# Block 0's attention sums as float32 products on TensorE, with a new order of all operations

## The chip, the cores and the metric

The kernel runs on one core of a Trainium2 chip. The core has a matrix engine (TensorE, called PE; its weight loads are shown apart as PEld), three engines for elementwise work (VectorE or DVE, ScalarE or ACT, GpSimd or POOL), and SyncE (SP), which here only issues DMAs. SBUF is the memory on the chip in which tiles lie, over 128 partitions; PSUM is the smaller one into which PE writes its products. Each engine runs its own list of instructions in order and waits on semaphores for the others. The metric is the time of one execution on the device in microseconds (us).

## The reference

Three steps follow one another on 8192 tokens (2 batches of 4096) of width 192:

```python
# 1: causal local attention, 7 taps, 8 heads of 24 channels
w = softmax(weight_gen, axis=-1)                     # per token and head, over the 7 taps
x_pad = concat([zeros(B, 6, D), x], axis=1)
out[b, s, h, :] = sum_k w[b, s, h, k] * x_pad[b, s + k, h*24:(h+1)*24]
# 2: h = x @ w_in (192 -> 2048); x = silu(h) @ w_out (2048 -> 192)
# 3: h = x @ w_in2
P = a0 + a1*h + a2*h**2 + a3*h**3
Q = 1 + |b0|*|h| + |b1|*h**2
out = (P / (Q + 1e-6)) @ w_out2
```

The weights of the two MLPs arrive as 64-bit floats.

## The kernel before, in words

**Tiling.** Token 64p + j lies on partition p at position j. The work is cut into 16 blocks of 4 positions, 512 tokens each. A block b goes through attention, MLP 1 (eight units, two hidden tiles of 128 each), and MLP 2 (the same). Numbers are split into a rounded part and a rest ("hi", "lo"), both in the format fp32r, and a product of two is made of three or so of their products.

**The order.** Every operation has a name and sits in one long list, ORDER, from which the program is issued; the order on each engine is the order of the list. `name@1` picks the second of the engines that the operation may run on, `:c` names the slot that its new tile takes (25 slots in SBUF, four of two banks each in PSUM, named A to D), and `^` marks ahead of a name load one of four function tables on ACT. Nothing else decides the order.

**Names.** X.b loads x's window of 10 positions for block b (Z.0 is the second half of block 0's: positions of the block itself; X.0 alone is the six positions that precede it, from the partition before). s0l, s0m, s0d, s0e, s0t, s0n are load, maximum, subtraction, exponential, sum and normalization of the softmax of a chunk of weights; s1 is the next chunk. For each position j, M (taps 0 to 3, 768 wide) and m (taps 4 to 6, 576 wide) multiply x by the weights (L580), p and r add (576 and 384 wide, L590 and L594), and a makes the last sum, 192 wide, into the tile ao (L600). AD copies the last 64 channels of ao beside themselves; T transposes ao to channels-by-tokens in PSUM (L628, L630); XH and XL make the hi and lo parts (L654, L658). In block 0 two groups of transposes whose results are overwritten run on PE as well: W0 (64, L635), which needs x, and W1 (16, L613), which needs a0 and ends ahead of the first multiplication, since A0.0 takes the same PSUM tile.

**The MLPs.** A0 to A7 and C0 to C7 are the two products of MLP 1 by unit, S, H and L its elementwise steps (silu, hi, lo); B, D, and U, V, u, w, Y, N, G, g, h, l are those of MLP 2; EC, EM, EA and FC, FT, FE, FA, O carry a block from MLP 1 to MLP 2 and out. A0.0 is thus the first multiplication of the MLPs; each unit's A has ten matmuls, six with the hi part of x (the second needs the lo part of the weights, q0A0x) and four with the lo part.

**The weights.** An operation name that begins with q is a step of decoding a weight tile: q0A0l0 and l1 load (MLP 0, matrix part A, tile 0), a0 and a1 and 40 and 41 put the number together from its 16-bit words on ACT (L448) and DVE (L461), h and x make hi (L477, L499) and lo (L482). All of it happens in the first 80 us, in between the rest.

Of the kernel before, what the change touches and what calls it, by code (L numbers as in the profile page):

```python
# [29 lines left out]
K = 7  # L30
# [19 lines left out]
    q1B0a1 q1B040:B a0.1:o X.2 C4.0 q1A1l1:b S6.0 q1B041 s3l:d a3.1 q0O3x q1A0a0 q1O3l1:m p1.1@1 q1B0h0 H6.0:g  # L50
    q1B0x0 a2.1 s2n@1 q1A0a1 L6.0:r A7.0:D q1B0h1 r1.1@1 s2s C5.0 q1O2l0:c q1A040:A a1.1 S7.0 q1A041 q1B0x1 C6.0
    H7.0:j q1O0a0 L7.0:e q1O0a1 AD.1@1 T.1:B q1A0h q1O040:D q1O041 C7.0 q1O1a0 q1A0x q1O0h q1O1a1 q1O0x XH0.1:q
    q1O140:A EC.0:w q1O141 EM.0 XL0.1:y A2.1:D q1O1h q1A1a0 q1O1x AW.2 q1A1a1 q1O3l0:p q1A140:B A1.1:A AW.3 S2.1
    q1A141 q1A1h@1 H2.1:s m3.2:u L2.1:n S1.1 M3.2:x q1O2a0 EA.0 A0.1:D H1.1:g q1A1x M2.2:r XH1.0:h L1.1:o A3.1:B
# [5 lines left out]
    L5.1:m H4.1:u r0.3@1 A6.1:D S7.1 L4.1:r m2.3:b H7.1:o Y3.0 p2.3@1 B4.0:C S6.1 L7.1:k g0.0 a3.2 C4.1 ^^U4.0:q  # L60
    h2.0@2:y N3.0 AD.2 h0.0@2:b B6.0:A V4.0:l Y1.0 H6.1:x u4.0 N1.0 C5.1 l0.0@1:r w4.0 M3.3:u L6.1:t T.2:C ^^^G3.0
    C6.1 U6.0:f g3.0 XH0.2:m Y4.0 G1.0 D0.0:D g5.0 g1.0 ^^^^s3e C7.1 XL0.2:n h1.0:e V6.0:t l1.0@1:x A0.2:C EC.1@1:c
    u6.0 EM.1 ^^N4.0 l2.0@1:b w6.0 D1.0 ^S0.2 h5.0:r H0.2:a EA.1 B7.0:A XH1.1:k L0.2:o XL1.1:s A3.2:C V7.0:p
    h3.0@2:e U7.0:x l3.0@1:c B1.1:B u7.0 S3.2 w7.0 D2.0 ^^^V1.1:h Y6.0 G4.0 H3.2:i B2.1:A g4.0 Y7.0 h4.0:j D3.0
# [5 lines left out]
    w5.1 ^S4.2 m1.4:o M2.4@1:t A6.2:A S7.2 r2.3@1 H7.2:j m2.4:v C3.2 S6.2 L7.2:m p1.4@1 H4.2:n B7.1:C L4.2:o h3.1:b  # L70
    ^^^G0.1 a2.3 r1.4 G2.1 C4.2 g0.1 H6.2:i Y5.1 h0.1:g V7.1:a B6.1:D g2.1 U7.1:n r0.4@1 G1.1 L6.2:o C5.2 AD.3 g1.1
    ^^N5.1 u7.1 B4.1:A h1.1:w U6.1:h p2.4@1 w7.1 V6.1:d C6.2 U4.1:p r2.4@1 Y6.1 V4.1:k l0.1@1:s T.3:C h2.1@1:v u6.1
    C7.2 XH0.3:i w6.1 N6.1 a0.4:o XL0.3:e D0.1:D M3.4:f u4.1 ^^^G6.1 l1.1@1:y EC.2@1:j A3.3:C G5.1 w4.1 EM.2 g5.1
    A0.3:A ^S3.3 g6.1 h5.1:m H3.3:g EA.2 D1.1 L3.3:s XH1.2:l l2.1@1:q S0.3 XL1.2:d H0.3:j B0.2:C Y4.1 l3.1@1:w
# [838 lines left out]
```

## Time and profile before

| | us |
|---|---|
| median of 3 runs | 1238.34 (1237.13 to 1238.6) |
| profiled execution | 1237.37 |
| its span (first to last instruction) | 1235.6 |
| PE busy | 1208.8 (98%) |
| ACT busy | 1107.3 (90%) |
| DVE busy | 1061.5 (86%) |
| POOL busy | 703.7 (57%) |

The profile is of one execution. Busy times of engines overlap each other. The view by stretches gives each engine's busy time between two moments, with the number of instructions; what PE lacks to the length of the stretch is its idle time. In a timeline a row gives the start, the time from the start to the end of the last of the merged instructions, the engine, the line of the kernel, the operation, and the tiles; in brackets stands the idle time ahead of it and what ended it. Instructions of one engine overlap a little, so that the distance from start to start is shorter than a row's own time.

### The profile page before, as it was taken

To read this page: it belongs to the slowest core of one execution; us is meant where nothing else is said; L and a number is where in the kernel's file an instruction comes from. 1 tells how busy PE (TensorE), PEld (TensorE's weight loads), DVE (VectorE), ACT (ScalarE), POOL (GpSimd) and SP (SyncE) were. 2 spreads that over 40 slices of the span, in tenths; PEclk is the share of its full clock that TensorE was granted. 3 is DMA by queue.
4 is the path that set the end of the run, shared out by engine and by line. 5 is a ranking of instruction groups with operands and counts; after the bars stand their busy time and mean duration, and the time that the engine had idled before them with its cause. 6 is when DMAs were issued, how large, how long until landed. Compare 5 with 4: busy or idle time off the path is not lost.

```text
span 1235.6 us, 14545 instructions
## 1 busy us (share of the span) xinstructions
PE 1208.8 (98%) x5456; PEld 997.3 (81%) x5456; DVE 1061.5 (86%) x954; ACT 1107.3 (90%) x1053; POOL 703.7 (57%) x455
## 2 busy tenths in 40 slices
...
DMA packets 18998, 45.15 MB, mean 37 GB/s; under 512 B 3828, under 2 KB 10354, under 8 KB 18928
## 3 DMA queue, kind: packets, MB, share of 16 engines
...
q8 instruction: 43, 0.70, 0.2%
q14 instruction: 27, 0.22, 0.1%
...
## 4 chain that ended last, share of the span: by engine, by line
PE 86%; DVE 6%; ACT 5%; issue 2%; DMA 1%; POOL 1%; SPq 0%; ACTq 0%; DVEq 0%; POOLq 0%
PE h L678 43%; PE acc L709 8%; PE acc L705 8%; PE acc L710 8%; PE acc L706 8%; PE acc L707 8%; ACT L878 1%; PE to L834 1%; DVE y L786 1%; DVE g1l L730 1%; ACT y L791 1%; ACT y L794 1%; ACT y L771 1%; DVE t L777 1%; DVE dec L461 1%
## 5 line engine op out<-in xcount | busy, mean ns | idle before, releaser
L807 POOL TENSOR_TENSOR g2l<-t,g2h 128x1024 fp32r<-128x1024 f32 x95 | 247.4, 2611 | 162.8 <-DVE g2h L317 93.7
L678 PE MATMUL h<-xh,wa 128*128 128x512 f32 x1024 | 317.7, 391 | 4.3 <-DVE g1l L730 1.8
L315 POOL TENSOR_SCALAR g2h<-t 128x1024 fp32r<-128x1024 f32 x84 | 108.7, 1298 | 232.2 <-DVE t L797 209.3
L678 PEld LDWEIGHTS h<-xh,wa 128*128 128x128 f32 x1024 | 190.4, 188 | 49.3 <-issue 4.2
L878 ACT ACT_TABLE_LOAD x167 | 214.3, 1283 | 3.7 <-PEq L897 0.7
L786 DVE SCALAR_TENSOR_TENSOR y<-y,b_sb 128x1024 f32<-128x1024 f32 x128 | 185.8, 1459 | 22.9 <-ACT y L771 22.6
L678 PE MATMUL h<-xl,wa 128*128 128x512 f32 x512 | 199.4, 389 | 0.4 <-DVE xl L658 0.4
L678 PE MATMUL h<-xh,wb 128*128 128x512 f32 x512 | 199.4, 389 | 0.0
L678 PE MATMUL h<-xl,wb 128*128 128x512 f32 x512 | 199.3, 389 | 0.0
L730 DVE TENSOR_TENSOR g1l<-h,g1h 128x1024 fp32r<-128x1024 f32 x128 | 155.6, 1219 | 46.0 <-ACT g1h L726 42.7
L777 DVE TENSOR_TENSOR t<-t,h 128x1024 f32<-128x1024 f32 x128 | 155.3, 1214 | 39.9 <-ACT t L767 26.1
L797 DVE SCALAR_TENSOR_TENSOR t<-t,a_sb,y 128x1024 f32<-128x1024 f32 x128 | 174.5, 1378 | 16.2 <-ACT y L794 15.9
L580 POOL TENSOR_TENSOR pr<-xw,aw 128x768 f32<-128x768 f32 (+1 forms) x99 | 153.2, 1558 | 32.6 <-DMA aw<-wsm 10.9
L780 DVE SCALAR_TENSOR_TENSOR t<-t,a_sb,h 128x1024 f32<-128x1024 f32 x128 | 163.5, 1279 | 8.2 <-ACT y L771 4.9
L722 ACT ACTIVATE h<-h 128x1024 f32<-128x1024 f32 x128 | 129.5, 1012 | 40.1 <-PE h L678 34.9
L767 ACT ACTIVATE t<-h,a_sb 128x1024 f32<-128x1024 f32 x128 | 153.4, 1202 | 13.1 <-PE h L678 11.9
L771 ACT ACTIVATE y<-h,b_sb 128x1024 f32<-128x1024 f32 x128 | 141.9, 1112 | 20.0 <-PE h L678 14.1
L791 ACT ACTIVATE y<-y,c_sb 128x1024 f32<-128x1024 f32 x128 | 144.4, 1148 | 10.5 <-DVE y L786 9.8
L726 ACT ACTIVATE g1h<-h 128x1024 fp32r<-128x1024 f32 x128 | 131.1, 1027 | 6.4 <-POOL ao L600 1.3
L794 ACT ACTIVATE y<-y 128x1024 f32<-128x1024 f32 x128 | 131.0, 1054 | 0.6
L678 PEld LDWEIGHTS h<-xl,wa 128*128 128x128 f32 x512 | 96.1, 188 | 20.9 <-DVE xl L658 0.9
L678 PEld LDWEIGHTS h<-xh,wb 128*128 128x128 f32 x512 | 96.1, 188 | 20.3
...
## 6 DMA issues: line engine op xcount, KB each, us to landing
...
```

Of the source, the lines that this page charges most:

```text
L580: e.tensor_tensor(out=p.rearrange("p k (h g) -> p k h g", g=G), in0=st[xw][:, j + k0:j + k0 + n, :].rearrange("p k (h g) -> p k h g", g=G) ...
L678: pe.matmul(out=h[:, i], lhsT=w[:, f], rhs=xx, start=(terms is first and n == 0), stop=(terms is second and n == 1),)
L730: dve.tensor_tensor(out=t, in0=st[hb], in1=st[gh].bitcast(F32), op=ALU.subtract)
L767: act.activation(out=q, in_=st[hb], func=AF.Identity, scale=a_sb[:, 3:4], bias=a_sb[:, 2:3])
L771: act.activation(out=q, in_=st[hb], func=AF.Abs, scale=b_sb[:, 1:2])
L777: dve.tensor_tensor(out=st[t], in0=st[t], in1=flat(), op=ALU.mult)
L780: dve.scalar_tensor_tensor(out=st[t], in0=st[t], scalar=a_sb[:, 1:2], in1=flat(), op0=ALU.add, op1=ALU.mult)
L786: dve.scalar_tensor_tensor(out=st[y], in0=st[y], scalar=b_sb[:, 0:1], in1=st[y], op0=ALU.add, op1=ALU.mult)
L791: act.activation(out=st[y], in_=st[y], func=AF.Ln, scale=c_sb[:, 0:1], bias=1e-6)
L797: dve.scalar_tensor_tensor(out=st[t], in0=st[t], scalar=a_sb[:, 0:1], in1=st[y], op0=ALU.add, op1=ALU.mult)
L807: e.tensor_tensor(out=q, in0=st[t], in1=st[gh].bitcast(F32), op=ALU.subtract)
L878: act.preload_act_table((None, AF.Silu, AF.Ln, AF.Sigmoid, AF.Exp)[k])
```

## The change

For block 0 the operations a, AD, T and W1 go. In their place K0 to K3 run on PE: for each position j, the two partial sums that r leaves are each multiplied by the identity in float32, and PSUM adds them. That gives the transposed sum in one step; the last 64 channels are multiplied twice, once for either half of the partitions, which is what AD's copy was for. A K operation has two products with 128 columns of weights and four with 64. W0 gets 24 transposes instead of 64. X.0 loads each of its two runs of 63 rows with two DMAs (48 and 15 rows) instead of one; the same code is used for X.1. The list ORDER is another one from its first line to its last. In it q0B0l0 goes ahead of X.0, m1.0 follows M0.0 on DVE, s0n goes to DVE and s0d to POOL, q0A0x stands directly ahead of XL0.0, K0.0 comes behind r0.0 and r0.0 behind s1d on POOL, T.1 goes behind C7.0, FT.14 goes ahead of D7.15. It has 182 loads of a function table instead of 167.

```diff
 ORDER = """
-    cn s0l X.0 Z.0 q0B0l0:a q0B0l1:b s0m s0d ^^^^s0e q0O0l0:c s0t q0A0l1:d q0A0l0:e s0n@1 cz:f M0.0@1:g M2.0:h
-    q0O0l1:i M1.0@1:j W0.0:A q0O1l1:k m3.0@1:l M3.0@1:m s1l q0B0a0 m0.0@1:n q0O1l0:o m1.0@1:p q0B040:B p3.0 q0B0a1
-    p1.0 m2.0@1:q q0B041 q0B0h0 p0.0 r0.0 q0B0h1 r1.0 p2.0 a0.0@1:r r2.0@1 r3.0 q0A0a1 X.1 q0A0a0 a1.0 a2.0@1 a3.0@1
-    q0O3l0:s q0A040:C AD.0 q1O1l1:t T.0 q0A041 q0A1l0:u q0B0x1 q0A0h s2l:v q0O0a1 q0B0x0 cl q0O0a0 XH0.0:w q0O040:D
-    s1m q0A0x W1.0:B s1d@1 s1e q0O2l1:x q0O1a0 q0O041 XL0.0:y A0.0 q0O0h q0A1l1:a q0O1a1 s1t q0O2l0:l q0O140:C
...
-    D4.15 Y7.15 ^^N7.15 g6.15 h6.15@2:o D5.15 u7.15 l6.15@1:d ^^^G7.15 w7.15 FC.14:t D6.15 g7.15 h7.15@2:b l7.15:n
-    D7.15 FT.14:C FC.15:l FE.14 FT.15:D FA.14 O.14 FE.15@1 FA.15 O.15
+    cn s0l q0B0l0:a X.0 cz:b s0m s0d@1 Z.0 ^^^^s0e q0A0l0:c s0t q0O0l0:d q0B0l1:e q0B0a0 s0n s2l:f q0A0l1:g M2.0:h
+    M0.0@1:i s1l q0O1l1:j W0.0:A m1.0@1:k cl M1.0@1:l m2.0@1:m m3.0@1:n p2.0 m0.0@1:o q0O0l1:p q0B040:B q0A0a0 r2.0
+    K2.0 p1.0 q0B0a1 M3.0@1:q X.1 p0.0 r1.0 K1.0 q0B041 q0B0h0 p3.0 q0A040:C q0A0a1 r3.0 q0O0a0 s1m K3.0 q0A041
+    q0B0h1 s1d@1 q0O1l0:r q0O040:D r0.0@1 q0O2l0:s q0A1l0:t q0O0a1 q0B0x0 q0A1l1:u K0.0 q0A0h q1A0l0:v q0B0x1
+    q1O0l0:w q1O1l1:x q0O041 q0A0x XH0.0:y q1B0l0:m s1e XL0.0:a A0.0:B q0O0h q0O1a0 q0O0x q0O2l1:k q0O1a1 q0O140:C
...
+    D6.15 FC.14:s g7.15 FT.14:A h7.15@2:t l7.15:y D7.15 FE.14@1 FA.14 FC.15:f O.14 FT.15:C FE.15 FA.15 O.15
 """
...
-WARM = (64, 16)
+WARM = (24, 16)
...
                 pool.memset(t[i * q:i * q + 1, 0:n, :], 0.0)
-                sp.dma_start(
-                    out=t[i * q + 1:(i + 1) * q, 0:n, :],
-                    in_=x_t[i * q:(i + 1) * q - 1, J - n:J, :],
-                )
+                for r0, r1 in ((0, 48), (48, q - 1)):
+                    sp.dma_start(
+                        out=t[i * q + 1 + r0:i * q + 1 + r1, 0:n, :],
+                        in_=x_t[i * q + r0:i * q + r1, J - n:J, :],
+                    )
...
+        def sums(j):
+            c = slice(j * P, (j + 1) * P)
+
+            def run(e):
+                t, p = st[tp], st[(*pr, j, 0)]
+                for k in range(2):
+                    pe.matmul(out=t[:, 0, c], lhsT=p[:, k, 0:P], rhs=ident, start=k == 0, stop=k == 1)
+                for h in range(2):
+                    for k in range(2):
+                        pe.matmul(
+                            out=t[h * DL:(h + 1) * DL, 1, c], lhsT=p[:, k, P:D], rhs=ident, start=k == 0, stop=k == 1,
+                        )
+            return run
...
+            if b == 0:
+                plan.op(f"K{j}", b, "PE", sums(j), rd=[*pt, (*tp, 0), ("ident", 0)], wr=[(*tp, 1 + j)])
+                continue
             plan.op(f"a{j}", b, "POOL DVE", add2, rd=[*pt, (*ao, 0)] if j else pt, wr=[(*ao, j)])
...
-        if b == 0:
-            plan.op("W1", b, "PE", warm_h, rd=[at[0], ("ident", 0), (*tp, 0)], wr=[("h", 0, 0, 0, 0)])
         split_x(0, b, tp)
```

## Rows read from the trace of the kernel before

**Rows 1.** The page: busy us (share of the span) and instructions of each engine.
```profile
PE 1208.8 (98%) x5456; PEld 997.3 (81%) x5456; DVE 1061.5 (86%) x954; ACT 1107.3 (90%) x1053; POOL 703.7 (57%) x455
```

**Rows 2.** By stretches: from:to, length, busy by engine (instructions), PE's clock, DMA share, GB/s.
```profile
29.33:80.00 50.67, 47.83 (x209) 37.86 (x208) 46.52 (x64) 46.98 (x59) 30.24 (x24) 1.00 0.62 182
80.00:200.00 120.00, 118.90 (x527) 96.66 (x526) 108.21 (x98) 115.89 (x110) 88.21 (x60) 1.00 0.08 27
200.00:1100.00 900.00, 900.00 (x4069) 745.73 (x4068) 768.94 (x663) 811.80 (x757) 527.89 (x332) 1.00 0.08 25
1000.00:1100.00 100.00, 100.00 (x455) 83.00 (x454) 82.46 (x70) 92.67 (x87) 38.78 (x26) 1.00 0.04 9
1100.00:1228.40 128.40, 126.04 (x556) 102.53 (x555) 112.59 (x95) 118.29 (x112) 47.03 (x23) 1.00 0.03 9
```

**Rows 3.** Timeline of PE in the head: W0, three of T.0's transposes, and W1.
```profile
9.60 8.59 PE L635 MATMUL tp<-ident,xw 128*128 128x128 f32 x64 [9.60 <-DMA xw<-in_x_dram]
...
21.81 0.55 PE L628 MATMUL tp<-ident,ao 128*128 128x128 f32 x3 [2.02 <-POOL ao L600]
...
25.66 3.68 PE L613 MATMUL h<-ident,ao 128*128 128x128 f32 x16 [1.99 <-DVE wb L482]
```

**Rows 4.** Timeline of DVE in the head, eight of its instructions.
```profile
7.48 0.96 DVE L580 TENSOR_TENSOR pr<-xw,aw 128x768 f32<-128x768 f32 x1 [2.34 <-DMA xw<-in_x_dram]
8.36 2.30 DVE L580 TENSOR_TENSOR pr<-xw,aw 128x768 f32<-128x768 f32 x1
10.58 0.75 DVE L580 TENSOR_TENSOR pr<-xw,aw 128x576 f32<-128x576 f32 x1
...
17.92 0.55 DVE L594 TENSOR_TENSOR pr<-pr 128x384 f32<-128x384 f32 x1
...
19.33 1.36 DVE L594 TENSOR_TENSOR pr<-pr 128x384 f32<-128x384 f32 x1
20.61 0.34 DVE L600 TENSOR_TENSOR ao<-pr 128x192 f32<-128x192 f32 x1
...
25.53 0.55 DVE L461 SCALAR_TENSOR_TENSOR dec<-raw,tops 128x384 int32<-128x384 int32 x1
...
28.01 1.22 DVE L658 TENSOR_TENSOR xl<-tp,xh 128x1024 fp32r<-128x1024 f32 x1
```

**Rows 5.** Timeline of POOL in the head: M2.0 and r2.0.
```profile
7.51 2.33 POOL L580 TENSOR_TENSOR pr<-xw,aw 128x768 f32<-128x768 f32 x1 [0.72 <-DMA xw<-in_x_dram]
...
19.22 1.05 POOL L594 TENSOR_TENSOR pr<-pr 128x384 f32<-128x384 f32 x1 [9.38 <-DVE pr L590]
```

**Rows 6.** By stretches of the head, columns as in rows 2.
```profile
0.00:8.00 8.00, 0.00 (x0) 0.00 (x0) 2.22 (x6) 1.67 (x2) 4.72 (x11) 1.00 0.69 156
...
3.00:4.00 1.00, 0.00 (x0) 0.00 (x0) 0.66 (x2) 0.27 (x1) 0.41 (x1) 1.00 0.61 215
23.00:24.00 1.00, 0.67 (x4) 0.26 (x2) 0.97 (x2) 0.85 (x1) 0.00 (x0) 0.50 0.94 373
```

**Rows 7.** The chain that ended last: four transposes of a later block's T.
```profile
120.61 0.44 PE tp L628 x4
```

**Rows 8.** By stretches, S0.0 to XH0.1's end, XL0.0's end to XL0.1.
```profile
31.82:68.50 36.68, 35.48 (x158) 28.44 (x156) 32.83 (x43) 35.53 (x45) 23.78 (x20) 1.00 0.70 201
29.23:69.36 40.13, 38.88 (x173) 31.25 (x173) 36.11 (x52) 37.54 (x47) 24.60 (x20) 1.00 0.70 209
```

**Rows 9.** Groups by line and form, first 40 us: hi of an O tile on DVE.
```profile
L479 DVE TENSOR_SCALAR wo<-dec 128x768 fp32r<-128x768 f32 x1 | 0.9, 946 | 0.0
```

**Rows 10.** The page's costliest groups: busy us, mean ns, idle before.
```profile
L878 ACT ACT_TABLE_LOAD x167 | 214.3, 1283 | 3.7 <-PEq L897 0.7
```

**Rows 11.** Timeline of the end: D7.15's first matmul, FE.14 on ACT, FE.15 on DVE.
```profile
1225.77 0.50 PE L705 MATMUL acc<-g2h,wo 128*128 128x512 f32 x1 [0.81 <-DVE g2h L317]
...
1229.35 0.81 ACT L313 ACTIVATE of<-to 128x768 f32<-128x768 f32 x1
...
1230.64 0.96 DVE L317 COPY of<-to 128x768 f32<-128x768 f32 x1
```

More of the change, by code (lines that the diff above doesn't have):

```diff
@@ L50 @@
[L50 to L54, printed above, removed]
@@ L60 @@
[L60 to L64, printed above, removed]
@@ L70 @@
[L70 to L74, printed above, removed]
@@ new lines @@
+    B6.9:D H7.10:h m1.12@1:i AD.11@2 L7.10:d C6.10 a0.12:m ^^V6.9:v Y5.9 U6.9:p FT.8:A Y6.9 N4.9 C7.10 h0.9@2:j
+    FE.8@1 N5.9 l0.9@1:n u6.9 N6.9 D0.9:B FA.8 EC.10@1:d w6.9 EM.10 ^^^G5.9 T.11:A O.8 g3.9 B7.9:D AW.13 XH0.11:h
+    h3.9:s G4.9 EA.10 l3.9@1:j D1.9 U7.9:n XL0.11:g XH1.10:u M1.12@1:l V7.9:w A0.11:A XL1.10:d X.13 p1.12@1 u7.9
+    B0.10:C ^S0.11 Y7.9 H0.11:b D2.9 L0.11:f V0.10:a w7.9 A1.11:A Y0.10 ^^N7.9 N0.10 g4.9 D3.9 U0.10:r r1.12
+    h4.9@2:i u0.10 l4.9@1:o A2.11:D w0.10 ^^^G7.9 a3.12 g5.9 B2.10:C ^S1.11 h5.9:q H1.11:x r2.12@1 D4.9 U2.10:j
@@ new lines @@
+    FC.10:q L3.12:w h1.11:x G0.11 B6.11:D V5.11:y g0.11 U5.11:e h0.11@2:b A4.12:B U6.11:f u5.11 l0.11@1:s w5.11
+    C3.12 ^S4.12 l1.11@1:n u6.11 H4.12:v A6.12:A V6.11:i L4.12:l M1.14:m w6.11 A5.12:B S6.12 g2.11 H6.12:d Y6.11
+    C4.12 S5.12 H5.12:w B4.11:D L5.12:a ^^N6.11 Y5.11 A7.12:B m3.14:p L6.12:l V4.11:v N5.11 r2.14@1 C5.12 U4.11:h
+    h2.11:u u4.11 T.13:A w4.11 ^S7.12 C6.12 M3.14:a H7.12:w Y4.11 L7.12:c D0.11:D ^^^G5.11 M0.14@1:d XH0.13:l
+    FT.10:B XL0.13:b C7.12 l2.11@1:s FE.10@1 ^^N4.11 g5.11 D1.11 EC.12@1:o h5.11:c ^^^G4.11 EM.12 m1.14:w B7.11:A
@@ new lines @@
+    B7.12:D V6.12:l w4.12 h1.12@1:t U6.12:d C6.13 l1.12@1:j AD.14@1 u6.12 V7.12:p D0.12:A U7.12:e Y6.12 r1.15@1
+    w6.12 N6.12 C7.13 a0.15:x N4.12 m2.15@1:a h3.12:y u7.12 l3.12@1:f T.14:B w7.12 D1.12 ^^^XH0.14:i EC.13@1:v G4.12
+    EM.13 XL0.14:m a3.15 G5.12 A1.14:D g4.12 G6.12 g5.12 A0.14:B EA.13 ^XH1.13:h g6.12 D2.12 h6.12@2:n S0.14
+    XL1.13:k l6.12@1:g H0.14:w M2.15@1:j S1.14 A2.14:C h4.12:t H1.14:b p2.15 D3.12 S2.14 L1.14:q r2.15@1 H2.14:v
+    L0.14:l l4.12@1:s B2.13:D Y7.12 h5.12:u D4.12 ^^V2.13:d L2.14:a U2.13:f l5.12@1:y B1.13:B N7.12 u2.13 w2.13
@@ L569, in weight, with warm_t @@
             return st["aw", b][:, j * HK:(j + 1) * HK].rearrange("p (h k) -> p k h", k=K)
+        def warm_t(e):
+            st[tp] = t = bank(tp, name="tp")
+            for _ in range(WARM[0]):
+                pe.transpose(out=t[:, 0, 0:P], in_=st[xw][:, K - 1, 0:P], identity=ident)
+        def sums(j):
[11 more added lines that the diff above has]
+        if b == 0:
+            plan.op("W0", b, "PE", warm_t, rd=[*xt, ("ident", 0)], wr=[(*tp, 0)])
         for j in range(JB):
```

344 lines of the change are left out of this document (167 added, 177 removed).

## The prediction, made before the changed kernel ran

> **What bounds the kernel now.** I read the page first: of the span of 1235.6 us TensorE (PE) is busy 1208.8 us, with ACT at 90%, DVE at 86% and POOL at 57% [rows 1]. A change can only take out time in which PE does no multiplication of the two MLPs. The view by stretches says where that is [rows 2]. From 200 to 1100 us PE is busy all 900.0 us, so nothing is to be had there and much is to be lost. Of 29.33 to 80 it stands 50.67 - 47.83 = 2.84 us, of 80 to 200 1.10, of 1100 to 1228.4 2.36: 6.3 us in all. The rest is the head, 29.33 us before the first multiplication, and the tail, 7.2 us behind the last.
>
> The head, by engine: PE waits 9.60 us for x, warms with W0, then has W1 at 25.66, 16 transposes in 3.68 us; so A0.0 begins at 25.66 + 3.68 = 29.34 [rows 3]. W1's own release is DVE's correction of the B weights (L482). DVE has hardly a gap from its first product of the attention at 7.48 to XL0.0 at 28.01 [rows 4]: the head is DVE's queue. Four of its rows carry what I need: the second product lasts 2.30 instead of 0.96 because POOL runs M2.0 beside it from 7.51 for 2.33 us [rows 4, 5]; a 384-wide sum lasts 1.36 instead of 0.55 beside POOL's own sum at 19.22 [rows 4, 5]. A POOL operation with two SBUF inputs stretches a DVE operation of that kind beside it.
>
> **The change, part by part.** Five things matter: X.0's load, DVE's list in the head, the K products, the work up to block 1, and the rest of the new order with the tail.
>
> *X.0.* Before, two DMAs of 283.5 KB are issued right behind s0l's 112 KB and release DVE at 7.48. Now q0B0l0's two DMAs (512 KB) go first, and X.0 is four DMAs. What must have moved when X.0 has landed is 112 + 512 + 567 = 1191 KB, 1.22 MB. Before, 156 GB/s over the first 8 us [rows 6] make 1.25 MB, so at the old pace it lands at 7.8. In 3 to 4 us, when X.0 was what the queue worked on, the DMA engines' share was only 0.61 [rows 6]; a better split over them would land it near 7.3, and with the two additional issues and no better split 8.5 is the other bound. I take 7.7. The Trainium skill, "DMA: Bandwidth & Descriptors", "Why a DMA increments its semaphore by 16 and not by 1", gives the rule: the number of rows has to be divisible by the number of engines, so 63 rows go over 9, and 48 and 15 over 16 and 15. The row's 0.61 is near 9/16, so the trace agrees; by the rule the early end, 7.3, would hold and the sum would be 0.4 us lower.
>
> Z.0 (384 KB, 0.39 MB, at the 215 GB/s of that stretch 1.85 us) follows at 9.55. The new order puts m1.0, which needs Z.0, second on DVE. POOL's M2.0, 2.33 us from 7.7, ends at 10.03. So DVE is back at 10.0 with one product done; before, it had two done at 10.58 [rows 4]. A product takes 0.88 from start to start (7.48 to 8.36; the next begins 0.08 before the 0.96 are over), so the same point comes at 10.88, 0.3 later (bounds -0.1 and 1.1).
>
> *DVE's list to XL0.0.* It is the same seven products, four p, three r, six joins, the corrections and s1m, without a0, a2 and a3 (0.34 each [rows 4], less the 0.08: -0.8). POOL's part is r0 and s1d where it was r2, a1 and AD.0; at 0.8 us of stretch for the first (1.36 against 0.55) and about half of that for each of the others I call them equal. Net 0.3 - 0.8 = -0.5: XL0.0 starts near 27.5. q0A0x, the correction without which the second multiplication of A0.0 can't run, now stands directly ahead of it and ends then too.
>
> *K products, W0, W1.* W1 is gone, and with it what held PE until 29.34. In place of a, AD and T.0, PE makes six products for each position j. The last, K0.0, needs r0, which waits on POOL behind s1d, and s1d behind s1m on DVE. Between s1m and XL0.0 DVE still has three joins (0.55) and three corrections (1.2) [rows 4], 5.3 us, with some 1.3 of stretch: s1m ends near 20.9, s1d (224 wide, so about 0.6 of the 384-wide 1.05 [rows 5]) and r0 (1.05) end near 22.5. Nothing in the trace is a float32 product that is not a transpose. The nearest row is block 1's T, four in 0.44 us at full clock [rows 7]; the far one is W1, 0.23 each at the half clock [rows 3]. Six make 0.7 to 1.4, or, taking each as long as two of W1's, 2.8. At the far end K0.0 is done at 25.3 and XH0.0 at 26.3, still ahead of 27.5. So I cost K at nothing; its cover is q0A0x. If the products last until 27.0, XH0.0 is the later one and A0.0 starts behind 28.
>
> *The clock.* Before, W0 ended at 18.2, PE stood nearly still to 21.8 [rows 3] and had a granted clock of 0.50, the lower of its two levels (1.2 of 2.4 GHz), in 23 to 24 [rows 6]; W1 ran at that, and A0.0 behind it at full clock. Now nothing warms it but K. K2 can begin near 15.4 (seven operations of DVE, 0.7 each from start to start, stand between 10.0 and r2), K0 at 22.5 and the two others between, so PE works in turns through to 23 to 25 and A0.0 follows 2 to 4 us later. I take full clock at A0.0 as more likely than not. Were A0.0 at half clock for as long as W1 was, 3.68 us, half of that time, 1.8 us, would be lost.
>
> So A0.0's stream begins at 27.5 - 0.2 (its first multiplication needs no q0A0x) = 27.3, against 29.34: **-2.0 us** (bounds -2.6 and 0). XL0.0 ends at 28.7 (1.22 [rows 4]); the seventh multiplication, the first that reads it, comes six times 0.22 (4069 PE instructions in 900 us [rows 2]) after 27.3, at 28.6. No wait to speak of.
>
> *From A0.0 to block 1.* What PE waits for next is XH0.1 and XL0.1. Between S0.0 and XH0.1 ACT is busy 35.53 of 36.68 us [rows 8]; the new order has the same operations there, but EC.0 for one q0O2h. So ACT's end moves with S0.0, 2 us earlier. DVE up to XL0.1 is busy 36.11 of 40.13 [rows 8] and gets more: p1, p2 (0.75 each, as the 576-wide row at 10.58 [rows 4]), r2 (0.55), q0O2h (0.95 [rows 9]), about 3.0 us in all with small ones, while POOL loses the same ones, which stretched DVE. DVE's 4.0 us of idle, mostly waits for ACT, and that relief cover most of it. XL0.1 comes some 1.4 us earlier than before instead of 2.0: **+0.6** given back (bounds 0 and 2.0).
>
> *The rest.* The order to the end is another one in detail: 15 more loads of ACT's tables (182 for 167, 1283 ns each [rows 10]: 19 us), and on DVE, in place of POOL, 12 M, 12 m and 6 p more, from 0.88 down to 0.67 each, some 23 us. Over the 1199 us that is 1.6% more of ACT, 90% to near 91%. From 1000 to 1100 ACT was busy 92.67 of 100 us and PE all of them [rows 2], so the level itself doesn't stop PE. I take **0** (bounds -2.5, when most of the 3.46 us of idle behind 80 go, and +4, when a tenth of these 42 us reaches PE).
>
> *The tail.* FT.14 goes ahead of D7.15, into the 0.81 us that PE waits there [rows 11]; it was behind FC.15 anyway, so that brings nothing. FE.15 goes to ACT: 0.81 for 0.96 [rows 11]: **-0.15**.
>
> **Sum.** -2.0 + 0.6 + 0 - 0.15 = -1.55. The profiled execution took 1237.37, its span 1235.6 and 1.8 around it; the median of the runs is 1238.34, 0.97 above it. So 1235.8 for an execution like the profiled one, and 1236.8 for the median. A measurement of this kernel can tell about 0.2%, 2.5 us, from no change; the forecast lies inside.
>
> **Rivals.** *The order also clears the old waits.* The 6.3 us of idle have a few causes (XH/XL of block 1, L2.1, the last two units). If more than half go, and the start is as forecast, it is -2.0 - 2.2 - 0.15 = 1234.0. For it: they are few, and all lie where ACT's and DVE's order decides. Against: DVE has more work in that place.
>
> *The head brings nothing.* Products as long as four of W1's transposes would take K0.0 5.5 us, from 22.5 to 28.0, XH0.0 to 29.0, and A0.0 starts as before; or PE is at half clock at A0.0, -2.0 + 1.8. Either gives 1238.2: with nothing gained ahead, nothing is given back, and the tail's 0.15 is left. The Trainium skill, "TensorE: Matmul & The Clock Gate", "Terms", says that transposing mode is four times as fast for float32: by that rule the first form would be real at the half clock; at the full clock it gives 2.6 us and nothing changes. No row here shows such a product.
>
> *ACT becomes the bound.* A table load in front of an operation that PE waits for within a block, where the slots in PSUM leave a wait no room: it decides from 1.55 + 2.5 = 4.1 us on, a fifth of the 19; with a fourth, 4.8, the time is 1238.34 - 1.55 + 4.8 = 1241.6. For it: ACT has 88 us of idle in 900 and the loads are spread over blocks 4 to 8. Against: 92.67% without a wait.
>
> **Chances.** Forecast 0.43 (range 1235.4 to 1238.2), waits cleared 0.28, head without gain 0.14, ACT the bound 0.15. Of the forecast's 0.43 some 0.07 lie below 1235.86. So faster by over 0.2%: 0.35; within: 0.50; slower: 0.15. The range reaches from the second case's far half, 1233.2, to a mild form of the last, 1239.8.
>
> **What would show it.** Right: A0.0's stream near 27.3 with a granted clock at 1.00, XL0.0 starting near 27.5, K0.0 done before 25.3, PE idle from there to 80 near 3.5 us, none from 200 to 1100, FE.15 on ACT. Wrong: X.0 later than 8.5; XH0.0 behind q0A0x; a clock of 0.50 at A0.0; new PE waits in the middle.

## The result and the profile after

The changed kernel takes 1246.51 us in the median of 4 runs (1246.0 to 1247.96), the kernel before 1238.46 beside it (1237.13 to 1238.6): 8.05 us more in the medians; the ratio run by run is 1.0072, 95% interval 1.006 to 1.0084. The forecast was 1236.8 with a range up to 1239.8. The profiled execution after took 1247.96, its span is 1246.2 against 1235.6.

The page's first part, busy time by engine, stands against [rows 1]: PE has 2.8 us more, DVE 28 and ACT 17 more, POOL 73 less.

```profile
PE 1211.6 (97%) x5440; PEld 995.6 (80%) x5440; DVE 1089.2 (87%) x1001; ACT 1124.7 (90%) x1063; POOL 630.9 (51%) x403
```

The view by stretches, with the columns of [rows 2]:

```profile
30.30:33.70 3.40, 3.40 (x10) 2.65 (x9) 3.24 (x9) 1.85 (x3) 0.29 (x1) 0.50 1.09 322
33.70:60.00 26.30, 26.30 (x116) 21.29 (x115) 24.54 (x32) 22.85 (x28) 17.62 (x15) 1.00 0.72 181
60.00:80.00 20.00, 15.60 (x68) 11.38 (x67) 18.65 (x26) 18.29 (x25) 7.93 (x7) 1.00 0.54 171
200.00:700.00 500.00, 498.32 (x2245) 411.37 (x2244) 443.88 (x385) 458.19 (x425) 282.82 (x175) 1.00 0.09 28
718.00:732.00 14.00, 11.57 (x49) 9.27 (x48) 11.69 (x11) 10.46 (x10) 9.84 (x6) 0.88 0.08 29
```

PE idles 4.40 us from 60 to 80, 1.68 from 200 to 700 and 2.43 in the 14 us around 725; before, it had 2.84 from 29.33 to 80 and nothing between 200 and 1100 [rows 2]. And twice, at 30.3 and around 727, PE is busy but at a granted clock of 0.50, the lower level.

A sharper measure is the lag: how much later than in the kernel before the n-th multiplication of the MLPs begins, worked out from the two traces. Multiplications are counted from 0, and the points lie where the changed kernel and the one before have the same transposes ahead of them (but for block 0's, and for FT.14 in the last column, which now fills the wait ahead of D7.15). It is the yardstick for the experiments, too.

| start of multiplication no. | 70 (45.9 us before) | 330 (111) | 2860 (700) | 3240 (788) | 5110 (1226) |
|---|---|---|---|---|---|
| forecast | -2.0 | -1.4 | -1.4 | -1.4 | -1.4 |
| changed kernel | 0.7 | 3.0 | 6.0 | 10.2 | 11.0 |
| h1: new head, order of before | 1.6 | 1.7 | 6.1 | 6.1 | 5.6 |
| h2: old head, changed order | 0.4 | 2.4 | 6.8 | 11.0 | 12.0 |
| b2: X.0 first, AD.10 on SP | -0.8 | 1.6 | 4.3 | 5.5 | 6.5 |
| b3: 15 more loads, order of before | 0.9 | 1.6 | 5.7 | 6.0 | 8.5 |
| d1: 15 loads fewer by nine moves | 1.0 | 3.3 | 8.7 | 12.9 | 22.1 |
| b4: new head mended, order of before | -1.6 | -1.6 | -1.6 | -1.7 | -2.2 |

The tail gives 0.4 back, so 11.0 - 0.4 = 10.6, the difference of the spans. A lag compares one execution with one: the profiled execution after lies 1.45 above its median and the one before 1.1 below, which is why 10.6 stands against 8.05 in the medians. b3 has block 0 as it was before and yet a lag of 0.9 at multiplication 70; s1, with the list of before, waits 1.40 us at one place in the middle in its profiled execution. So a difference of lags of 1 to 1.5 us counts only where the trace shows the place it comes from.

**The head**, timeline of DVE, then of PE [rows 4, 3]:

```profile
9.69 3.84 DVE L602 TENSOR_TENSOR pr<-xw,aw 128x768 f32<-128x768 f32 x3 [2.86 <-DMA xw<-in_x_dram]
...
24.87 2.46 DVE L482 SCALAR_TENSOR_TENSOR wb<-dec,wb 64x1024 fp32r<-64x1024 f32 x2 [1.21 <-ACT wb L499]
...
27.96 1.22 DVE L482 SCALAR_TENSOR_TENSOR wa<-dec,wa 128x1024 fp32r<-128x1024 f32 x1
29.10 1.22 DVE L671 TENSOR_TENSOR xl<-tp,xh 128x1024 fp32r<-128x1024 f32 x1
```

```profile
25.10 0.71 PE L583 MATMUL tp<-ident,pr 128*128 128x128 f32 x4 [0.94 <-POOL pr L616]
25.74 0.66 PE L586 MATMUL tp<-ident,pr 128*64 128x128 f32 x8
27.54 0.50 PE L690 MATMUL h<-xh,wa 128*128 128x512 f32 x1 [1.13 <-ACT xh L667]
29.23 0.50 PE L690 MATMUL h<-xh,wa 128*128 128x512 f32 x1 [1.20 <-DVE wa L482]
...
30.65 0.63 PE L690 MATMUL h<-xl,wa 128*128 128x512 f32 x1
31.08 0.63 PE L690 MATMUL h<-xl,wb 128*128 128x512 f32 x1
```

X.0 releases DVE at 9.69, not at 7.7. The last K product is done at 26.4 and XH0.0, which follows it, before q0A0x (L482): K is hidden, but q0A0x comes at 29.2 and holds the second multiplication. From 30.3 a multiplication takes 0.43 from start to start (31.08 - 30.65) instead of 0.22.

**In the middle**, the only waits of PE from 120 us to 718 that are over 0.2 us, timeline of PE (A1.6, B6.6, B7.6):

```profile
437.84 0.70 PE L690 MATMUL h<-xh,wa 128*128 128x512 f32 x2 [0.61 <-DVE xl L671]
...
569.66 0.73 PE L690 MATMUL h<-xh,wa 128*128 128x512 f32 x2 [0.50 <-DVE g1l L741]
...
578.96 0.70 PE L690 MATMUL h<-xh,wa 128*128 128x512 f32 x2 [0.42 <-DVE t L791]
```

A1.6 waits for XL0.6, the two others for a PSUM tile that L or w frees. Those at B6.6 (0.50 to 0.53) and B7.6 (0.37 to 0.42) stand in the traces of a1 to a4, b2, d1, d2 and h2 as well; the one at A1.6 goes there from nothing (a4, h2) to 1.35 (d2).

**Around 726**, timeline of DVE, POOL and PE:

```profile
720.23 2.20 DVE L317 COPY ao<-ao 128x256 f32<-128x256 f32 x1
722.35 2.43 DVE L797 SCALAR_TENSOR_TENSOR y<-y,b_sb 128x1024 f32<-128x1024 f32 x1
724.70 1.27 DVE L791 SCALAR_TENSOR_TENSOR t<-t,a_sb,h 128x1024 f32<-128x1024 f32 x1
...
719.87 2.40 POOL L818 TENSOR_TENSOR g2l<-t,g2h 128x1024 fp32r<-128x1024 f32 x1
722.22 1.47 POOL L612 TENSOR_TENSOR pr<-pr 128x576 f32<-128x576 f32 x1
...
726.12 0.77 PE L690 MATMUL h<-xh,wa 128*128 128x512 f32 x2 [2.43 <-DVE t L791]
```

AD.10, before a DMA, is now a copy on DVE. It ends only when POOL's operation beside it does (722.43 and 722.27); Y5.8 (L797) behind it is stretched too, so w4.8 (L791), which frees B6.8's PSUM tile, comes 2.43 us too late.

**The tail** [rows 11]: FE.15 is on ACT with 0.81 as forecast, and from the last MLP multiplication to the end of the span it is 7.27 us (1238.93 to 1246.2) instead of 7.66 (1227.94 to 1235.6). Of this 0.4 FE.15 gives 0.14 (0.85 instead of 0.99 from its start to FA.15's); 0.25 is the last store, 3.71 instead of 3.96 us from FA.15's start to the end.

```profile
1239.36 1.02 ACT L313 ACTIVATE of<-acc 128x1024 f32<-128x1024 f32 x1 [4.23 <-PE acc L721]
...
1241.62 0.81 ACT L313 ACTIVATE of<-to 128x768 f32<-128x768 f32 x1 [1.24 <-PE to L845]
```

### The profile page after: what moved, and what is told of

Same layout as the page of the kernel before. It is cut to its first block, busy times and chain, and to the rows that moved or that the text cites. A ratio compares the mean times of both kernels' runs of the same rounds, so it can differ in the third digit from the quotient of the medians.

```text
span 1246.2 us, 14547 instructions
## 1 busy us (share of the span) xinstructions
PE 1211.6 (97%) x5440; PEld 995.6 (80%) x5440; DVE 1089.2 (87%) x1001; ACT 1124.7 (90%) x1063; POOL 630.9 (51%) x403
## 4 chain that ended last, share of the span: by engine, by line
PE 80%; ACT 6%; DVE 5%; issue 2%; DMA 0%; POOLq 0%; POOL 0%; DVEq 0%; ACTq 0%
PE h L690 40%; PE acc L720 8%; PE acc L721 8%; PE acc L716 8%; PE acc L717 8%; PE acc L718 8%; ACT L889 1%; ACT y L802 1%; PE to L845 1%; ACT y L782 1%; ACT y L805 1%; DVE y L797 1%; ACT t L778 1%; DVE t L808 1%; DVE t L788 1%
## 5 line engine op out<-in xcount | busy, mean ns | idle before, releaser
L315 POOL TENSOR_SCALAR g2h<-t 128x1024 fp32r<-128x1024 f32 x69 | 90.7, 1317 | 274.8 <-DVE t L808 238.2
L797 DVE SCALAR_TENSOR_TENSOR y<-y,b_sb 128x1024 f32<-128x1024 f32 x128 | 176.6, 1389 | 13.7 <-ACT y L782 13.3
L808 DVE SCALAR_TENSOR_TENSOR t<-t,a_sb,y 128x1024 f32<-128x1024 f32 x128 | 173.4, 1369 | 11.0 <-ACT y L805 10.8
L788 DVE TENSOR_TENSOR t<-t,h 128x1024 f32<-128x1024 f32 x128 | 155.2, 1214 | 30.3 <-ACT t L778 18.4
L791 DVE SCALAR_TENSOR_TENSOR t<-t,a_sb,h 128x1024 f32<-128x1024 f32 x128 | 163.3, 1278 | 3.7 <-ACT y L782 0.7
L782 ACT ACTIVATE y<-h,b_sb 128x1024 f32<-128x1024 f32 x128 | 142.0, 1112 | 19.4 <-PE h L690 16.1
L602 POOL TENSOR_TENSOR pr<-xw,aw 128x768 f32<-128x768 f32 (+1 forms) x75 | 112.0, 1503 | 40.9 <-DMA aw<-wsm 17.7
L690 PEld LDWEIGHTS h<-xl,wb 128*128 128x128 f32 x512 | 96.7, 189 | 20.2
```

The source lines that it names most:

```text
L690: pe.matmul(out=h[:, i], lhsT=w[:, f], rhs=xx, start=(terms is first and n == 0), stop=(terms is second and n == 1),)
L782: act.activation(out=q, in_=st[hb], func=AF.Abs, scale=b_sb[:, 1:2])
L788: dve.tensor_tensor(out=st[t], in0=st[t], in1=flat(), op=ALU.mult)
L791: dve.scalar_tensor_tensor(out=st[t], in0=st[t], scalar=a_sb[:, 1:2], in1=flat(), op0=ALU.add, op1=ALU.mult)
L797: dve.scalar_tensor_tensor(out=st[y], in0=st[y], scalar=b_sb[:, 0:1], in1=st[y], op0=ALU.add, op1=ALU.mult)
L808: dve.scalar_tensor_tensor(out=st[t], in0=st[t], scalar=a_sb[:, 0:1], in1=st[y], op0=ALU.add, op1=ALU.mult)
```

## The experiments

The kernel before took 1237.5 to 1238.3 us in the median beside these runs; each ratio is to the runs beside it.

**Head or rest?** Two hybrids: the changed list up to A0.0 with the order of before behind it (h1; 51 slots had to be other ones, and four loads of MLP 2's weights stand behind A0.0, as before), and the reverse with the code of before (h2; 32 other slots).

```diff
 h1:  ... XL0.0:a A0.0:B | q0O0h ...      changed up to here, before from here
 h2:  ... XL0.0:y A0.0   | q0O0h ...      before up to here, changed from here
```

> The changed code with the changed order up to A0.0, then before's order for all that is left. If the head's own loss is small and the rest of the new order carries most of the 8 us: 1238.5 to 1240.5, with A0.0's second matmul near 29.2 as in the changed kernel. If the late head is what throws the rest out of step: 1244 or more.

> Before's code and order up to A0.0, then the changed order for all that is left. If the rest of the new order carries most of the loss: 1243 to 1246. If the head does: 1238 to 1239.5.

h1: 1242.84, ratio 1.0039 (1.0025 to 1.0054). h2: 1249.07, ratio 1.0089 (1.0074 to 1.0104). The changed order behind A0.0, without anything of the change in block 0, loses more than the whole change does, and more than the 1243 to 1246 expected. The new head costs too, with a time between the two that were expected; h1 also loses 4.4 us between 111 and 700 us, 3.0 of them as waits at A3.2, D0.1 and B0.2 (0.77, 0.86, 1.41), which this run can't part from its changed slots.

**The split and the products by themselves**, each in the kernel before:

```diff
 s1:  -  dma(t[i*q+1:(i+1)*q], x_t[...])            +  for r0, r1 in ((0, 48), (48, q - 1)): dma(...)
 k1:  -  a0.0 a1.0 a2.0 a3.0 AD.0 T.0 W1.0          +  K0.0 K1.0 K3.0 K2.0, each behind its r
```

> Before with nothing but X.0 and X.1 in four DMAs (48 and 15 rows). If the split over more DMA engines is what counts, DVE's first product starts at 6.3 to 6.9 instead of 7.48 and the time falls by 0.4 to 1.0 us, 1237.4 to 1238.0. If it is the bytes ahead in the queue alone: 7.3 to 7.7 and 1238.4 within 0.5.

> Before's order with K0 to K3 in place of a, AD, T and W1 of block 0, W0 with 64 transposes, X.0 in two DMAs. If the products are hidden behind q0A0x as argued, A0.0's second matmul comes 1.0 to 2.0 us earlier than 29.6, and with the clock at full the time is 1236.5 to 1237.5; with a half clock behind A0.0 it is 1238 to 1239. If the products are on the path: 1239 or more.

s1: 1236.61, ratio 0.9987 (0.9977 to 0.9996); DVE's first product begins at 6.85 where it was 7.48 [rows 4]. By the Trainium skill, "DMA: Bandwidth & Descriptors", "Why a DMA increments its semaphore by 16 and not by 1", 63 rows go over 9 engines. The 0.63 us earlier start agrees, and so do the traces' DMA records: X.0's packets keep 0.57 of the 16 engines busy from 3 to 5 us in the kernel before, and over 0.9 of them from 5 to 7 us in the changed one. The time fell by 1.65 us in the medians, more than the 0.4 to 1.0 expected. k1: 1237.41, ratio 0.9994 (0.9984 to 1.0003). A0.0 begins at 26.5, 2.5 us earlier, but at half clock from 27.1, and at the third unit it is 1.4 late in its trace. Neither part is slower by itself; neither explains the loss.

**X.0's landing, and block 10's copy.**

```diff
 a1:  -  cn s0l q0B0l0:a X.0 cz:b          +  cn s0l X.0 q0B0l0:a cz:b
 a2:  -  C6.9 AD.10@2 Y5.8                 +  C6.9 AD.10@3 Y5.8
 b2:  both
```

> The changed kernel with X.0's four DMAs issued ahead of q0B0l0's 512 KB; nothing else is changed. Theory A (the start of DVE's list is late because q0B0l0 goes first): M0.0 begins near 7.0 us instead of 9.7, as in the kernel before with X.0 split (6.9); q0A0x ends some 1.5 to 2.5 us earlier than 29.2, and if the clock stays full the time falls from 1246.5 to about 1244. Rival R (the head is not DVE's list alone, or what is gained there is given back in block 1): M0.0 is early all the same, but the time falls by less than 0.7 us.

> The changed kernel with the copy of block 10's last 64 channels (AD.10) as a DMA on SP instead of an instruction of 2.2 us on DVE; nothing else is changed. Theory A (the step of +4 us at 726 us is DVE's list: AD.10, Y5.8, w4.8 ahead of B6.8, and the half clock of 3.4 us is a result of that wait of 2.4): no wait ahead of B6.8, no half clock there, lag behind the kernel before stays near 5.5 us instead of 10, time near 1242.5. Rival R1 (a wait and a half clock come back somewhere behind, or Y5.8 is as late, beside POOL's l0.8): the lag reaches 9 us anyhow, time 1245 to 1247. Rival R2 (the half clock at 726 is not caused by the wait): no wait, but half clock near 726 and 1.7 us lost.

> The changed kernel with both of the shown remedies: X.0's DMAs ahead of q0B0l0 (worth 1.7 us of lag in its profile, less in the median) and AD.10 as a DMA on SP (worth 2.8 us). If they are two separate causes, the sum holds: lag of some 6.5 us at the end in place of 11, time 1242 to 1243.5. If PE gives back behind block 1 what the head gains, time 1244 or above.

a1: 1246.16, ratio 1.0063 (1.0051 to 1.0076), by itself not told apart from the changed kernel by its time. In its trace the head goes as theory A says, timeline of DVE:

```profile
6.87 0.96 DVE L598 TENSOR_TENSOR pr<-xw,aw 128x768 f32<-128x768 f32 x1
...
25.61 1.23 DVE L478 SCALAR_TENSOR_TENSOR wa<-dec,wa 128x1024 fp32r<-128x1024 f32 x1
26.75 1.21 DVE L667 TENSOR_TENSOR xl<-tp,xh 128x1024 fp32r<-128x1024 f32 x1
```

So q0B0l0's place costs X.0 2.8 us and XL0.0 2.35. The lag is 1.6 to 1.7 less from multiplication 70 on (-0.9 there), to the end (9.3); the rest of the 2.35 goes at A0.0, as the lower clock holds there from 25.1 to 31.9 us.

a2: 1244.73, ratio 1.0056 (1.0044 to 1.0069), an interval that overlaps the changed kernel's. Timeline of DVE and PE:

```profile
720.47 3.12 DVE L793 SCALAR_TENSOR_TENSOR y<-y,b_sb 128x1024 f32<-128x1024 f32 x1
723.51 1.27 DVE L787 SCALAR_TENSOR_TENSOR t<-t,a_sb,h 128x1024 f32<-128x1024 f32 x1
...
724.92 0.70 PE L686 MATMUL h<-xh,wa 128*128 128x512 f32 x2 [1.00 <-DVE t L787]
```

The wait falls from 2.43 to 1.00: Y5.8 begins 1.9 us earlier, but is now itself stretched to 3.12 beside POOL (its form has 1.39 in the mean of 128). The half clock is gone, and the lag at the end is 8.2. But a4 below kept the wait at B6.8, 2.43 us as in the changed kernel, and had no half clock there, so that part is not shown to follow from the wait.

b2: 1243.44, ratio 1.0042 (1.0029 to 1.0055); lag 6.5. The two add up: 11.0 - 1.7 - 2.8 = 6.5, and the ratio is the only one of the three whose interval lies below the changed kernel's. They are separate causes, and 6.5 us of lag remain.

**Block 1 and the clock at A0.0.**

```diff
 a3:  -  C7.0 ... T.1:C q1O1a1 EC.0 ... XH0.1     +  T.1:C C7.0 ... XH0.1 q1O0h ... EC.0
 a4:  +  the first matmul of A0.0 seven times more (start=True, overwritten)
 d2:  -  s1n@1 m3.1@1 q0O2h@1 m2.1 p2.1 p1.1 s2n r2.1     +  s1n m3.1 q0O2h m2.1@1 p2.1@1 p1.1@1 s2n@1 r2.1@1
```

> The changed kernel with T.1 ahead of C7.0 on PE and XH0.1 ahead of q1O0h on ACT, as they stood in the kernel before; nothing else is changed. Theory A (the 2.2 us that the lag grows between 60 and 80 come from T.1 and XH0.1 standing late): XH0.1 ends near 69.5 instead of 71.3, A2.1 begins near 69.8 instead of 71.5, time near 1244.5. Rival R (XL0.1 on DVE is what decides, behind L7.0, q1A0x and the corrections, so the wait moves from the first to the seventh multiplication): A2.1 is earlier but ends as late, time within 0.7 us of 1246.5.

> The changed kernel in which the first multiplication of A0.0 is issued eight times in place of once (each overwrites the one before), so that PE has work while it waits for q0A0x; nothing else is changed. Theory A (the half clock from 30.3 to 33.7 follows PE's standing still between 26.5 and 29.2): PE works from 27.5 on, the half clock shrinks or goes, A1.0 begins up to 1.7 us earlier, time 1245 or a little less. Rival R (the clock is set by what lies further back, the K products with gaps from 14.7 to 26.5): half clock from about 30 all the same, no gain; if the repeats run at half clock, up to 1 us is lost, as eight take up to 3.5 us.

> The changed kernel with the eight operations of c2 on their former engines, all table loads left where they stood. If the lost 24 us of c2 behind block 1 come from the 45 loads that it moved: time some 20 us or more below c2's 1272.6, so 1246 to 1252, with the same lag of about 5.8 at A2.1. Theory A of c2 (DVE has too much in this stretch) has fallen if the lag at A2.1 is again above 4; it stands if it is near 1.5 (the loads' places changed before that point, too).

a3: 1247.97, ratio 1.0086 (1.0072 to 1.01), no gain. Timeline of PE:

```profile
68.50 0.63 PE L642 MATMUL tp<-ident,ao 128*128 128x128 f32 x4 [2.96 <-DVE g1l L737]
```

T.1 takes the PSUM tile that L7.0 frees, and L7.0 (on DVE) is as late as ever, so T.1's place behind C7.0 is not the cause. a4: 1247.16, ratio 1.0074 (1.006 to 1.0087). The eight issues ran at a clock of 0.50 from 28.5 on, the lower level lasted from 19.4 to 33.0, and the lag at multiplication 70 rose to 2.3: rival R. But the level fell 9 us ahead of the first repeat, and it stood at 0.50 from 19 to 33 in the traces of a2, a3, b1, d1 and d2 too, which have none; where it falls is not the same in each execution of this head. d2: 1249.34, ratio 1.0089 (1.0074 to 1.0104); with six operations off DVE and two onto it the lag at 330 is 3.4 against 3.0, and XL0.1 begins at 72.0 instead of 71.7. DVE's load is not what holds it; timeline of DVE in d2:

```profile
63.44 2.46 DVE L478 SCALAR_TENSOR_TENSOR wb<-dec,wb 64x1024 fp32r<-64x1024 f32 x2 [0.89 <-ACT wb L495]
```

DVE waits here for ACT's hi of a weight (0.89 us, in the changed kernel 0.60 ahead of 63.11), and from this correction's start to XL0.1's it is 8.60 us in either.

**DVE's list, ACT's loads.** In b1 the M, m, p, r of blocks 2 to 15 go back to their former engines; in b3 the kernel before gets 15 redundant loads.

```diff
 b1:  -  M2.3@1 M1.3@1 m3.4@1 ...  (59 on DVE, 27 on POOL)     +  the engine before for each, same places
 b3:  -  S3.1 S3.2 S5.3 ... S4.12 ... S3.15                    +  ^S3.1 ^S3.2 ^S5.3 ... ^S4.12 ... ^S3.15
```

> The changed kernel with the changed order, in which the M, m, p and r operations of blocks 2 to 15 run on the engine that they had in the kernel before: 59 go from DVE to POOL and 27 from POOL to DVE; nothing else is changed. Theory A (what is lost between 100 and 710 us, 2.2 us of lag, and in the wait of B6.8 at 726 comes from DVE, which the new order gives 12 M, 12 m and 6 p more): the lag at 710 us falls from 5.2 towards 3, time about 1244 to 1245. Rival R1 (it is the places of the operations in the order, not DVE's load): the lag at 710 us stays at 5 or more, time 1246 to 1249. Rival R2 (ACT's 15 additional table loads): no change in the middle either.

> The kernel before with 15 additional loads of ACT's function table, one ahead of a silu in each of the blocks 1 to 15, of the table that is loaded already; nothing else is changed. Rival (ACT becomes the bound, a fourth of the 15 x 1.28 us reaches PE): 4.8 us slower, about 1242.5. Theory A (ACT's slack and the PSUM slots hide the loads, the lost time of the changed kernel comes from elsewhere): within 1 us of the kernel before.

b1: 1256.85, ratio 1.0154 (1.014 to 1.0168), 10 us worse than the changed kernel and outside all that was expected. Moving them back, a net 32 off DVE, is no remedy: from 120 to 1160 us PE now waits eleven times for over 0.2 us instead of four, each time for DVE, the longest 2.30 at B6.4. What DVE's additional operations cost by themselves is not told by this, since the places in the list were made for the other engines. b3: 1245.89, ratio 1.006 (1.0047 to 1.0074), 8.1 us slower: the rival that I had priced at a fourth of the loads' time. 15 loads are 19.2 us, and 42% reached PE. One of them, timeline of ACT and PE in b3:

```profile
930.11 1.12 ACT L766 ACTIVATE y<-h,b_sb 128x1024 f32<-128x1024 f32 x1
931.25 1.28 ACT L873 ACT_TABLE_LOAD   x1
932.54 1.01 ACT L717 ACTIVATE h<-h 128x1024 f32<-128x1024 f32 x1
...
934.55 1.02 ACT L721 ACTIVATE g1h<-h 128x1024 fp32r<-128x1024 f32 x1
...
935.63 0.50 PE L700 MATMUL acc<-g1h,wo 128*128 128x512 f32 x1 [1.02 <-ACT g1h L721]
```

The load ahead of S4.12 makes silu and hi 1.28 later, and PE waits 1.02 for hi.

**Fewer loads in the changed order.** Nine operations were moved by one to four places of ACT's list, so that 167 loads are left.

```diff
 c1, d1:  moved  G7.4 N3.11 N4.8 N7.13 G5.7 N5.10 S0.8 G5.11 G6.9
 c1, c2:  also   45 loads from an operation that doesn't use the table (^U0.4) to the first that does
 c2:      d2 with these 45 loads moved as well
```

> The changed kernel with nine operations of ACT (G7.4, N3.11, N4.8, N7.13, G5.7, N5.10, S0.8, G5.11, G6.9) moved by one to four places of ACT's list, so that operations with one table stand together and 167 table loads are left instead of 182; nothing else is changed. Theory A (the 15 loads are the cause of much that is lost, as 15 of them in the kernel before cost 8 us, 0.54 each): 4 to 8 us faster than the changed kernel, 1239 to 1242.5. Rival R (the order was made with the loads, so PE waits for the moved operations in their new places instead): 1245 or more.

> The changed kernel in which eight operations of the stretch between A0.0 and block 1 run on the engine of the kernel before: m3.1, p1.1, p2.1, r2.1 and s2n on POOL, q0O2h on ACT (these six off DVE), m2.1 and s1n on DVE; nothing else is changed. Theory A (DVE has too much in this stretch): XL0.1 up to 1.5 us earlier, the lag behind the kernel before at A2.1 falls from 2.9 towards 1.5, time near 1245. Rival R (POOL beside DVE stretches DVE's operations, or ACT is what ends late): lag at A2.1 stays within 0.5 of 2.9, or grows.

> The changed kernel with the nine operations of c1 moved and 167 loads, all other loads left where they stood. Theory A (the number of loads costs: 15 in the kernel before cost 8 us): 4 to 8 us faster than the changed kernel, 1239 to 1242.5. Rival R (the order was made with its loads; the moved operations make PE wait in their new places, or the loads taken out were hidden): 1246 or more.

c1 took 1279.13 (1.0336, 1.0322 to 1.035), c2 1272.6 (1.0285, 1.0271 to 1.0299), and c1 with both remedies of b2 1272.63. All three carried a second edit that I had not meant: the 45 loads. So c1 says nothing of its theory; but c2 and d2 differ in those loads alone, with 182 in either, and are 23.3 us apart: a load moved from its early place to its user cost 0.52 us of the whole each. The likely reason is that ahead of an operation that waits anyway it is hidden: in d2 30 of the 182 loads are followed by an idle stretch of ACT of over 0.2 us, in c2 8.

d1, with the 45 in place, took 1259.01 (1.0166, 1.0152 to 1.0180), 12.5 us worse than the changed kernel. Timeline of ACT and PE in d1:

```profile
592.61 1.28 ACT L884 ACT_TABLE_LOAD   x1
593.90 1.01 ACT L728 ACTIVATE h<-h 128x1024 f32<-128x1024 f32 x1
...
597.28 0.73 PE L685 MATMUL h<-xh,wa 128*128 128x512 f32 x2 [1.83 <-DVE g1l L736]
```

S0.8 (L728), at 586.35 in the changed kernel, runs at 593.90 here, L0.8 is late, and B2.7 waits 1.83 for the tile. Further waits of this kind come ahead of C6.11 (2.1) and in D5.10 (1.7 and 1.2). Loads were saved, and places in the order lost. What the changed order's own 15 additional loads cost could not be told in this way.

**A version that beats both.** The order of before, in which X.0 stands ahead of the weights; X.0 in four DMAs; K products; two moves, q0A0x ahead of q0O040 and s1m and XH0.0 ahead of q0O0a1; ten transposes ahead of K2 and five repeats of A0.0's first matmul (b4), or without these fifteen (f1).

```diff
-    q0A041 q0A1l0 q0B0x1 q0A0h s2l q0O0a1 q0B0x0 cl q0O0a0 XH0.0 q0O040 s1m q0A0x W1.0
+    q0A041 q0A1l0 q0B0x1 q0A0h s2l XH0.0 q0O0a1 q0B0x0 cl q0O0a0 q0A0x q0O040 s1m
```

> The order of the kernel before, with X.0 ahead of the weights and in four DMAs, K0 to K3 in place of a, AD, T and W1 of block 0, W0 of 64 transposes, q0A0x directly behind q0B0x0 on DVE and XH0.0 directly behind q0A0h on ACT; ten transposes ahead of K2 and five repeats of A0.0's first multiplication keep PE at work. DVE loses a0, a2, a3 and the wait for its ACT inputs; q0A0x ends near 25.6 to 26.2 us and XL0.0 near 27 instead of 29.2. Theory A (the head is bounded by DVE's list; the new order behind it is what lost the time): A0.0 ends 1.5 to 3 us earlier than in the kernel before and 1 to 2 us of it last, time 1236 to 1237, below both kernels. Rival R (half clock at A0.0, or what is gained in the head is given back in block 1): 1237.5 to 1238.5.

> The kernel b4 without the ten transposes ahead of K2 and without the five repeats of A0.0's first multiplication; nothing else is changed. Theory A (the fill keeps the clock up): PE stands nearly still from 22.5 to 25.7 us, a granted clock of 0.50 begins between 22 and 28 us as in the products alone, and up to 1.8 us are lost: 1236 to 1237.2. Rival R (the fill does nothing, b4's gain is the earlier q0A0x and XL0.0): full clock or half as it falls, the time stays at 1235.3 within 0.5 us.

b4: 1235.32 (1235.06 to 1235.51, 11 runs), ratio 0.9979 (0.9970 to 0.9987), below the 1236 to 1237 expected. f1: 1235.54 (1234.9 to 1236.12), ratio 0.9977 (0.9966 to 0.9987). Timeline of DVE and PE in b4:

```profile
24.51 1.23 DVE L477 SCALAR_TENSOR_TENSOR wa<-dec,wa 128x1024 fp32r<-128x1024 f32 x1
...
26.88 1.22 DVE L668 TENSOR_TENSOR xl<-tp,xh 128x1024 fp32r<-128x1024 f32 x1
...
22.27 0.61 PE L580 MATMUL tp<-ident,pr 128*128 128x128 f32 x4
...
24.63 1.41 PE L688 MATMUL h<-xh,wa 128*128 128x512 f32 x5 [1.15 <-ACT xh L664]
```

By stretches, b4 and then f1, 23 to 30 us:

```profile
23.00:30.00 7.00, 5.09 (x27) 3.77 (x25) 6.89 (x13) 4.63 (x9) 0.90 (x2) 1.00 0.84 292
```

```profile
23.00:30.00 7.00, 4.97 (x11) 3.27 (x11) 6.89 (x13) 4.51 (x9) 0.93 (x2) 0.62 0.85 308
```

XL0.0 begins 1.1 us earlier than before [rows 4]; the 1.6 us of lag gained there are kept to the end, where it is 2.2. The fill holds the clock at the upper level (mean over the core 0.999 or more in all 11 runs; 0.997 or 0.998 in 7 of f1's 8), but the seventh multiplication, the first that reads XL0.0, begins at 28.15 in b4 and at 28.13 in f1, so up to there the fill gains nothing. The medians are alike.

## Why the prediction was wrong

**The step that failed most is "The rest": 0, with 4 as its worst.** It measured 8.0 of the lag's 11.0: 3.0 from 111 to 700 us, 4.2 around 726, 0.8 behind. That the order behind A0.0 loses by itself is shown by h2. I had argued that "the level itself doesn't stop PE" because ACT was busy 92.67 of 100 us without a wait [rows 2]. b3 refutes that: the mean share says nothing of slack, since a wait comes from one operation that is late, whatever the mean. Every disturbance of an order was paid for: 15 loads 8.1 us, 45 loads at other places 23.3, nine operations of ACT moved 12.5, 86 operations on other engines 10.3. My bound, a tenth of the added busy time, was four times too low for b3's loads (42%). Around 726 the cause is shown in part: AD.10 on DVE (a2, b2). For the other 5 us of this term the trace names where PE waits in the middle (A1.6, B6.6 and B7.6, 1.5 us together, all for DVE), but why DVE is late there was not tried; the changed order's 15 loads remain a candidate that no run here parts from their places.

**X.0's landing** was mis-sized: 7.7 forecast, 9.7 measured, outside the bound of 8.5. The pace was not the fault, as the stretch up to the landing shows [rows 6]:

```profile
0.00:9.69 9.69, 0.00 (x0) 0.00 (x0) 1.70 (x6) 2.45 (x3) 4.25 (x10) 1.00 0.78 177
```

The method was: to divide the bytes issued up to X.0 by the mean pace. For the kernel before it gives 112 + 567 KB, 0.70 MB, by 156 GB/s, 4.5 us, where 7.48 was measured. In the traces' DMA records X.0's last packet ends at 6.40 us before and at 8.53 after, and DVE begins 1.1 us later in either; the sum had no term for that. The split by itself does what was said (s1, 6.85); q0B0l0's 512 KB ahead of it takes it away and 2.2 us more (a1). DVE had two products done at 12.59 instead of 10.88; m1.0 didn't wait for Z.0 but was stretched to 2.10 beside M2.0. From there to XL0.0 two errors cancel, which is luck: no sum was stretched beside POOL (0.55 each instead of 1.36 [rows 4]), and a wait that I had missed, 1.21 us for ACT's hi of the B weights, took that up. So XL0.0 began at 29.10, 1.6 later than forecast. The gain was also counted from a row's modelled end: A0.0 began at 28.98 before and not at 29.34, so of the -2.0 only 1.7 was there.

**The clock at A0.0** was called full "more likely than not"; it was at 0.50 from 30.3 to 33.7, half of which, 1.7 us, is lost, near the 1.8 of the other bound. Together the head came to +0.7 instead of -2.0.

**From A0.0 to block 1**: +0.6 forecast, +2.3 measured (0.7 to 3.0), above the bound of 2.0. Taking DVE's additional operations away didn't help (d2). What failed is "ACT's end moves with S0.0"; by stretches, S0.0 to XH0.1's end, against [rows 8]:

```profile
32.60:71.35 38.75, 36.43 (x158) 28.82 (x157) 36.15 (x51) 34.89 (x45) 19.94 (x17) 0.99 0.71 195
```

S0.0 was 0.8 later instead of 2 earlier, and the stretch took 2.07 more with 0.64 less of ACT's work in it: ACT idles 3.86 us of it instead of 1.15, the longest waits being 1.15 and 0.82 for PE and 1.10 for DVE. In the end H7.0 is done at 66.1, behind two weight operations that now precede S7.0 on ACT (62.06 to 63.62), and C7.0 (0.84), A2.1 (1.20) and two units behind it (0.59, 1.36) wait in turn; this was read, not tried.

**Right** were K, hidden by q0A0x (k1; six products 1.3 us at full clock, about 2.3 at half, within 0.7 to 2.8), W1's and T's going, and FE.15 in the tail (0.14 for 0.15; the rest of the -0.4 is the last store's and was not forecast). Of the rivals, "ACT becomes the bound" had the right mechanism for the order of before (b3) with too low a price, 4.8 us for 8.1; the forecast, the waits cleared and the head without gain all took the order for neutral or better.
